# Seventeen more identity products on TensorE in the opening of a sorted-block attention kernel

## The chip, the cores and the metric

The kernel runs on one core of one Trainium2 chip. The metric is the device time of one execution in microseconds (us), as the median of several runs. A profile is one further execution, taken with its trace; times within it count from the first instruction.

## The reference, cut to what matters

Block-sorted attention, followed by a two-layer feed-forward part. The sorting matrix comes out of five rounds of row and column normalisation of `sort_net`; keys and values are mixed block by block with it; then each query block attends to its own sorted block.

```python
B, H, S, D = q.shape                       # 4, 8, 768, 64; 8 blocks of 96 rows
for _ in range(5):                         # P = sort_net, (4, 8, 8, 8)
    P = np.exp(P - np.max(P, axis=-1, keepdims=True))
    P = P / (np.sum(P, axis=-1, keepdims=True) + 1e-09)
    P = P / (np.sum(P, axis=-2, keepdims=True) + 1e-09)
k_sorted = np.einsum('bhij,bhjcd->bhicd', P, k_b)
v_sorted = np.einsum('bhij,bhjcd->bhicd', P, v_b)
scores = scale * np.matmul(q_b, k_sb.transpose(0, 1, 2, 4, 3))
attn = softmax(scores)                     # over the 96 keys of the block
x = np.matmul(attn, v_sb)                  # then (B*S, 512)
h = x @ w_in                               # 512 -> 2048
g = np.maximum(h, 0.0) + alpha * np.minimum(h, 0.0)
out = g @ w_out                            # 2048 -> 512
```

## The kernel before, in words

The work is cut into 32 pieces, g = 0 to 31: eight blocks in each of four batches. A piece is one block of 96 rows for all eight heads. Everything that the engines do is first recorded as operations in a graph (`G.add`), each with its engine, what it reads and what it writes. The order in which the engines take them is written out by hand: the table `SEQ` lists the numbers of all operations, and each engine runs its own in that order. `emit` then sets semaphore waits from the recorded reads and writes.

The opening of the program works on batch 0 (g = 0 to 7):

- `burst` (L888): 110 tiny products on zeros.
- `prep_q` (L600 on `hT`, which holds the loaded q of batch 0): six turnings of q into columns, evicted by ScalarE (ACT, L372) to `QTz`. The first is operation 89.
- `sinkhorn` on VectorE (DVE) and ACT gives the sorting matrix `Pb`; `spread0` (operation 79, L539) spreads it over the partitions, and L543 masks it to the block-diagonal `BDK`.
- `prep_k` (L600 on `KS`): six sorting products of k, evicted to `KT`; POOL pads `KT` (L642).
- `conv_v` (L653): copies on POOL and DVE that bring the loaded v into place in `hT`; `prep_v` (L674): eight sorting products of v, evicted to `VS`. The first is operation 114, the last operation 128.
- `attention(g)`: L715 (`s1`) makes scores, L721 takes their negated maxima `nm` on DVE; L736 and L727 (`s2`) make the turned scores and add `nm`; L759 exponentiates to `ET` on ACT; L768 (`o`) multiplies with `VS`; L776 and L779 divide on DVE to `xq`; L794 turns `xq`, and L372 evicts it to `xT`. Operation 158 is `s1` of g = 1; 162 is `o` of g = 1 (into `psYP`), 153 is `o` of g = 0 (into `psO`).

From then on the feed-forward part is woven in: `ffn1` (L823, `xT` times `w_in`, evicted by L833 and L836 to `hT`) and `ffn2` (L862, `hT` times `w_out`).

Beside this, the kernel has products whose result nobody reads: the identity matrix `identb` times itself repeated four times, 128 x 128 by 128 x 512, in bfloat16 (L808). The table `WARM` lists them: `89:10:y` puts ten ahead of operation 89 into the PSUM bank that the letter names (`y`: `psYP` at 0, `h`: `psH` at 0). `G.warm` inserts them into TensorE's order and has them wait for the identity, and for readers of the bank where there are any. Then comes the next entry of TensorE's order. All loads are issued by POOL; the queues of the other engines are not touched by `WARM`.

Of the kernel before, what the change touches and what calls it, by code (L numbers as in the profile page):

```python
# [29 lines left out]


WARM = """
89:10:y 79:7:y 93:2:y 104:2:y 114:7:y 158:2:y 153:2:h 205:1:y 207:1:y
"""

SEQ = """
# [993 lines left out]
```

## Time and profile before

| | |
|---|---|
| time, median of 3 runs | 239.45 us (238.71, 239.45, 241.29) |
| profiled execution, its own time | 238.55 us |
| its span, first to last instruction | 236.8 us |
| TensorE (PE) busy | 226.7 us, 96% of the span |
| DVE, ACT, POOL busy | 169.4, 151.7, 73.3 us |
| mean granted clock of PE | 0.992 |
| identity products (L808) | 38 |

The page gives busy time by engine, the span in forty slices, the chain that ended last, and groups of instructions by line. PE is the TensorE's products, PEld its weight loads. A row of the timeline has start, length, engine, line, operation, what is written and read, shapes and count; a bracket holds the idle time ahead of it and what ended it. The ends of products are modelled and include a tail, so that the next product may start ahead of a shown end.

### The profile page before, as it was taken

The page shows a single profiled execution, that of the slowest core. Times are in us where ns is not written, and L with a number is a line of the kernel's source. Part 1 is how long each engine was busy: PE and PEld are TensorE (multiplying, and loading weights), DVE is VectorE, ACT ScalarE, POOL GpSimd, SP SyncE. Part 2 cuts the span into 40 slices and gives each one's busy share as a digit, 9 for nine tenths or more (in the row PEclk, how much of TensorE's full clock was granted, in tenths as well). Part 3 has the DMA queues.
Part 4 walks back from the last instruction along what each step waited for, and adds up shares of the span by engine and source line. Part 5 has one row for each costly group of instructions (what it writes and reads, how often), then busy time and mean ns, then how long its engine had stood idle before and what let it go on. Part 6 is the DMA issues. An engine that isn't in the chain of part 4 may idle for free.

```text
span 236.8 us, 6180 instructions
## 1 busy us (share of the span) xinstructions
PE 226.7 (96%) x2474; PEld 142.7 (60%) x2503; DVE 169.4 (72%) x353; ACT 151.7 (64%) x423; POOL 73.3 (31%) x140
## 2 busy tenths in 40 slices
PE   7798899999999999999999999999999999999995
PEld 3346688687666666566655665655555555555544
DVE  4737688989899997869897667676766577644240
ACT  4465257587887988886768786756863646353232
POOL 7939824805879221148390020000000000000000
PEclk9999799999999999999999999999999999999999
DMA  5999999999999998999999797652442323400033
GB/s 95 214 214 212 205 219 195 173 212 162 181 92 145 141 168 125 154 182 194 130 100 92 210 157 157 98 95 42 125 106 69 97 50 84 132 3 0 1 136 133
DMA packets 70941, 31.36 MB, mean 132 GB/s; under 512 B 64504, under 2 KB 65280, under 8 KB 70912
## 3 DMA queue, kind: packets, MB, share of 16 engines
q0 software_dynamic: 22384, 13.63, 42.0%
q1 hardware_dynamic: 48528, 17.33, 36.9%
q8 instruction: 20, 0.33, 0.6%
q14 instruction: 9, 0.07, 0.1%
HBM read 27.28 MB, written 6.29 MB: 142 GB/s over the span
## 4 chain that ended last, share of the span: by engine, by line
PE 88%; DMA 5%; POOL 3%; DVE 2%; issue 1%; ACT 1%; POOLq 0%
PE psH L823 34%; PE psYP L862 30%; DMA VST<-in_v_dram 5%; PE psS L862 4%; PE psS L712 4%; PE psO L768 3%; PE psYP L669 2%; PE psYP L629 2%; PE psS L727 2%; PE psO L794 1%; PE psS L736 1%; PE psS L715 1%; POOL VDz L456 1%; POOL hT L653 1%; PE psH L808 1%
## 5 line engine op out<-in xcount | busy, mean ns | idle before, releaser
L836 DVE SCALAR_TENSOR_TENSOR hT<-t,omaT,psH 128x384 bf16<-128x384 f32 (+1 forms) x139 | 77.2, 571 | 36.3 <-ACT t L833 35.5
L823 PE MATMUL psH<-xT,w_in_bf 128*128 128x384 bf16 (+1 forms) x556 | 97.1, 311 | 0.0
L833 ACT ACTIVATE t<-psH 128x384 f32<-128x384 f32 (+1 forms) x139 | 62.9, 460 | 50.0 <-PE psH L823 47.7
L862 PE MATMUL psYP<-w_out_bf,hT 128*128 128x512 bf16 x308 | 77.6, 379 | 1.5
L823 PEld LDWEIGHTS psH<-xT,w_in_bf 128*128 128x128 bf16 x556 | 49.4, 98 | 29.4 <-DVE hT L836 2.1
L862 PEld LDWEIGHTS psYP<-w_out_bf,hT 128*128 128x128 bf16 x336 | 30.9, 98 | 28.2
L748 ACT ACTIVATE Esb<-psS,nf 96x96 bf16<-96x96 f32 x192 | 46.1, 345 | 2.0 <-DVE nf L721 2.0
L721 DVE TENSOR_REDUCE nf<-psS 96x8 f32<-96x768 f32 x24 | 22.8, 950 | 6.4 <-PE psS L712 6.0
L658 POOL COPY VDz<-VST 64x192 f32<-64x192 f32 x39 | 20.4, 523 | 19.2 <-DMA VST<-in_v_dram 13.5
L616 POOL COPY KSz<-KS 64x256 f32<-64x256 f32 x28 | 11.3, 404 | 33.6 <-PE psYP L629 21.2
L779 DVE TENSOR_TENSOR xq<-psO,rec 96x512 bf16<-96x512 f32 x31 | 21.2, 683 | 0.5
L401 POOL DMA_DIRECT2D QN<-in_q_dram x24 | 20.0, 838 | 2.3 <-DMA QTz<-QN 1.5
L712 PEld LDWEIGHTS psS<-KT,QTz 128*96 128x96 bf16 x192 | 12.1, 125 | 3.3
L768 PEld LDWEIGHTS psO<-VS,ET 112*128 112x128 bf16 x248 | 11.3, 99 | 3.9 <-ACT ET L759 0.5
L372 ACT ACTIVATE VS<-psYP 112x512 bf16<-112x512 f32 x15 | 10.3, 685 | 4.7 <-PE psYP L674 2.4
L768 PE MATMUL psO<-VS,ET 112*128 112x65 bf16 x248 | 13.0, 196 | 0.0
L712 PE MATMUL psS<-KT,QTz 128*96 128x96 bf16 x192 | 12.6, 208 | 0.0
L808 PE MATMUL psYP<-identb 128*128 128x512 bf16 x32 | 10.4, 460 | 0.5 <-ACT identb L372 0.5
L372 ACT ACTIVATE KT<-psYP 128x512 bf16<-128x512 f32 x15 | 8.9, 596 | 2.6 <-PE psYP L629 1.6
L372 ACT ACTIVATE outstg<-psYP 128x512 f32<-128x512 f32 x13 | 7.7, 604 | 3.2 <-PE psYP L862 3.2
L669 PEld LDWEIGHTS psYP<-BDV,VDz 128*128 128x128 bf16 x192 | 8.2, 98 | 2.4 <-ACT VS L372 0.2
L669 PE MATMUL psYP<-BDV,VDz 128*128 128x64 bf16 x192 | 9.5, 193 | 0.0
(137 smaller groups left out, 199.5 us busy)
## 6 DMA issues: line engine op xcount, KB each, us to landing
out_dram<-outstg SPq DMA_DIRECT2D x23, 256.0 KB, 2.4
KS<-in_k_dram POOLq DMA_DIRECT2D x3, 768.0 KB, 13.2
QN<-in_q_dram POOLq DMA_DIRECT2D x24, 96.0 KB, 4.7
w_in_bf<-in_moe_w_in_dram POOLq DMA_DIRECT2D x4, 512.0 KB, 16.0
w_out_bf<-in_moe_w_out_dram POOLq DMA_DIRECT2D x2, 1024.0 KB, 22.5
VST<-in_v_dram POOLq DMA_DIRECT2D x4, 384.0 KB, 17.2
hT<-in_q_dram POOLq DMA_DIRECT2D x1, 768.0 KB, 7.6
VST<-in_v_dram POOLq DMA_DIRECT2D x1, 768.0 KB, 11.5
```

The costliest lines, as they stand in the source:

```text
L372: return e.activation(o, i, ACTF.Copy) if e is nc.scalar else e.tensor_copy(o, i)
L658: G.add(SHIFT, lambda e, o2=o2, i2=i2: e.tensor_copy(o2, i2), {"dve": 424, "pool": 525}, r=vst, w=[("VDz", u % VSL, th)], prio=prio)
L669: inst = e.matmul(AP(t, off + dd * 64, [[row, 128], [1, 64]]), AP(VDz, (u % VSL * 4 + dd // 2) * 256 + dd % 2, [[VSL * 1024, 128], [2, 128]]),
L712: inst = e.matmul(o, AP(QTz[n], hp * 3072 + h4 * 768 + i * 96, [[6144, 128], [1, 96]]), AP(KT[n], (h4 * 8 + i) * bk, [[ld, 128], [64, 2], ...
L721: G.add(DVE, lambda e: e.tensor_reduce(AP(nx, 0, [[8, 96], [4, 2], [1, 4]]), AP(psX, 0, [[1024, 96], [512, 2], [96, 4], [1, 96]]), AxisLis ...
L748: inst = e.activation(AP(Esb[me], p * 128, [[1024, 96], [64, 2], [1, 48]]), AP(psX, (p // 4) * 512 + (p % 4) * 96, [[1024, 96], [48, 2], [ ...
L768: inst = e.matmul(AP(psZ, hp * 512 + h4 * 68, [[1024, 128], [1, 65]]), AP(ET[me] if far else ET[m], pos(h4, hp) * 96, [[800, nk], [1, 128] ...
L779: G.add(DVE, lambda e: e.tensor_tensor(out=AP(xq[me], 0, [[512, 96], [256, 2], [64, 4], [1, 64]]), in0=AP(psZ, 0, [[1024, 96], [512, 2], [ ...
L823: inst = e.matmul(AP(pt, poff, [[1024, 128], [1, n]]), AP(w_in_bf, kt * DFF + ft // 2 * 256 + ft % 2, [[KT_TILES * DFF, 128], [2, 128]]), ...
L833: G.add(ACT, lambda e: e.activation(AP(t1[tb], 0, [[384, 128], [1, n]]), AP(pt, poff, [[1024, 128], [1, n]]), ACTF.Relu, scale=-1.0), t_ac ...
L836: G.add(DVE, lambda e: e.scalar_tensor_tensor(out=AP(hT, ft * RING + tok % RING, [[FT_TILES * RING, 128], [1, n]]), in0=AP(t1[tb], 0, [[38 ...
L862: inst = e.matmul(AP(bank[0], bank[1], [[1024, 128], [1, n]]), AP(hT, ft * RING + tok % RING, [[FT_TILES * RING, 128], [1, 128]]), AP(w_ou ...
```

## The change

The counts of six places in `WARM` are raised, and two places are new. The operations, their data and the order of all others stay.

```diff
 WARM = """
-89:10:y 79:7:y 93:2:y 104:2:y 114:7:y 158:2:y 153:2:h 205:1:y 207:1:y
+89:14:y 79:8:y 93:2:y 104:2:y 114:9:y 158:6:y 153:3:h 205:1:y 207:1:y 128:4:y 162:1:y
 """
```

Four more stand ahead of operation 89, one more ahead of 79, two ahead of 114, four ahead of 158, one ahead of 153; new are four ahead of 128 and one ahead of 162: seventeen.

TensorE's order (the only one that differs), where v's first sorting product (L674) follows k's last (L600) and the first scores of g = 1 (L715) come; the names behind the operation are the tile written and the tiles read:

```order
 L600 MATMUL psH<-BDK,KS 64x64 x32
 L600 MATMUL psO<-BDK,KS 64x64 x32
-L808 MATMUL psYP<-identb 128x512 x7
+L808 MATMUL psYP<-identb 128x512 x9
 L674 MATMUL psO<-BDK,hT 64x64 x16
-L808 MATMUL psYP<-identb 128x512 x2
+L808 MATMUL psYP<-identb 128x512 x6
 L715 MATMUL psH<-KT,QTz 96x96 x8
 L674 MATMUL psYP<-BDK,hT 64x64 x16
```

Two more products stand ahead of L674 and four more ahead of L715. Further on, TensorE from v's last sorting products to the two output products (L768), before the change:

```order
L674 MATMUL psO<-BDK,hT 64x64 x48
L736 MATMUL psS<-QTz,KT 112x96 x8
L727 MATMUL psS<-identb,nm 112x96 x8
L768 MATMUL psYP<-VS,ET 128x65 x8
L808 MATMUL psH<-identb 128x512 x2
L768 MATMUL psO<-VS,ET 128x65 x8
L808 MATMUL psH<-identb 128x512 x4
```

and with it:

```order
L674 MATMUL psO<-BDK,hT 64x64 x32
L808 MATMUL psYP<-identb 128x512 x4
L674 MATMUL psO<-BDK,hT 64x64 x16
L736 MATMUL psS<-QTz,KT 112x96 x8
L727 MATMUL psS<-identb,nm 112x96 x8
L808 MATMUL psYP<-identb 128x512
L768 MATMUL psYP<-VS,ET 128x65 x8
L808 MATMUL psH<-identb 128x512 x3
L768 MATMUL psO<-VS,ET 128x65 x8
L808 MATMUL psH<-identb 128x512 x4
```

The last of v's three sorting products in this place now comes behind four identity products, the output product of g = 1 behind one, and that of g = 0 behind three instead of two.

## The prediction

> **What bounds the kernel now.** I read the page first: the shares of the engines, the clock that TensorE (PE) was granted in each fortieth of the span, and the shares of the chain that ended last.
>
> ```profile
> PE 226.7 (96%) x2474; PEld 142.7 (60%) x2503; DVE 169.4 (72%) x353; ACT 151.7 (64%) x423; POOL 73.3 (31%) x140
> PEclk9999799999999999999999999999999999999999
> PE 88%; DMA 5%; POOL 3%; DVE 2%; issue 1%; ACT 1%; POOLq 0%
> ```
>
> PE is the bound, and one slice out of forty, the fifth (23.7 to 29.6 us), has less than a full clock. The rest of the chain lies mostly in the opening. The chain in order of time, over the opening, shows what sets the pace there:
>
> ```profile
> 5.45 11.47 DMA VST<-in_v_dram
> ...
> 19.68 0.38 PE psH L715 x8
> ...
> 27.00 0.85 PE psH L808 x2
> ```
>
> Until 19.6 us the load of v and POOL's copies set the end; PE only fills waits. From 24.60 on the chain stays on PE, identity products (L808) among it. Busy time by stage, in stretches cut at the places where the clock changes, and at last the long rest:
>
> ```profile
> 18.00:21.41 3.41, 2.43 (x88) 1.74 (x83) 2.37 (x6) 1.31 (x3) 3.09 (x6) 1.00 1.04 211
> 21.41:24.82 3.41, 2.50 (x79) 2.14 (x75) 2.51 (x5) 2.18 (x3) 2.95 (x8) 1.00 1.05 210
> 24.80:24.85 0.05, 0.05 (x14) 0.05 (x10) 0.00 (x0) 0.00 (x0) 0.00 (x0) 0.75 0.81 164
> 28.20:28.25 0.05, 0.05 (x3) 0.04 (x1) 0.00 (x0) 0.00 (x0) 0.02 (x1) 0.62 1.89 369
> 32.00:232.00 200.00, 198.42 (x1868) 124.21 (x1895) 149.31 (x284) 136.56 (x391) 48.60 (x90) 1.00 0.78 123
> ```
>
> After the length of a row come PE, PEld, DVE, ACT and POOL; the third number from the end is the clock. A slice at 0.75 is half full and half at 0.50, so the clock falls to half at 24.825; by the 0.62 it is back at 28.24. That is 3.41 us at half speed, worth at most 1.71 us. From 32 to 232 us PE is busy 99% at full clock: nothing there swallows a shift, so what PE gains or loses by 32 us reaches the end one to one.
>
> **Fifteen of the seventeen products: do they fit in waits?** PE's timeline, with the wait ahead of a row in brackets:
>
> ```profile
> 2.80 4.45 PE L808 MATMUL psYP<-identb 128*128 128x512 bf16 x10 [0.53 <-ACT identb L372]
> 8.92 0.44 PE L600 MATMUL psS<-identb,hT 64*64 64x64 bf16 x16 [1.68 <-DMA hT<-in_q_dram]
> ...
> 10.55 1.69 PE L808 MATMUL psYP<-identb 128*128 128x512 bf16 x7
> 12.42 0.37 PE L539 MATMUL psYP<-Pb,sel 32*128 32x8 bf16 x8 [0.18 <-DVE Pb L532]
> ...
> 15.62 1.68 PE L808 MATMUL psYP<-identb 128*128 128x512 bf16 x7
> 16.95 0.34 DVE L653 COPY hT<-VST 128x192 f32<-128x192 f32 x1 [2.52 <-DMA VST<-in_v_dram]
> 17.70 0.45 PE L674 MATMUL psO<-BDK,hT 128*64 128x64 bf16 x16 [0.41 <-POOL hT L653]
> 18.09 0.60 PE L808 MATMUL psYP<-identb 128*128 128x512 bf16 x2
> 19.68 0.38 PE L715 MATMUL psH<-KT,QTz 64*96 64x96 bf16 x8 [0.98 <-POOL KT L642]
> ...
> 24.60 0.52 PE L674 MATMUL psO<-BDK,hT 128*64 128x64 bf16 x16 [0.88 <-DVE VS L372]
> ```
>
> Two products last 0.60 and seven 1.69, so one more costs (1.69 - 0.60)/5 = 0.218 us; of a run's shown time 0.16 is the tail of the last, which the next product does not wait for. The first ten (4.45) step by 0.425: the array runs at half speed there too, although the page shows 9 (its clock record has not begun). Place by place, with the tail added to the wait shown:
>
> - ahead of the first turning: 4 x 0.425 = 1.70, wait 1.68 plus tail, so 14 products from 2.80 leave the array at 8.75, q comes at 8.92.
> - ahead of L539: 0.22 against 0.18 + 0.16.
> - ahead of the first L674: 0.44 against 0.41 + 0.16.
> - ahead of L715: 4 x 0.218 = 0.87 against 0.98 + 0.16.
> - ahead of the last L674: 0.87 against 0.88 plus a tail.
>
> So all fifteen cost nothing at full clock, with 0.1 to 0.3 us left at each place; what hides them are DMAs, POOL copies and evictions, which don't depend on them. Were the cover gone at one place, it would cost 0.2 to 0.9. Only PE's order changes; no other queue is moved past anything.
>
> **What they do to the clock.** The trace has no record of what decides it, so I bound it. The stretch that ended in the fall holds as much busy PE time (2.50) as the one before it, which kept full clock (2.43); but the same stretches, with the identity products alone, read
>
> ```profile
> 18.00:21.41 3.41, 0.60 (x2) 0.11 (x2) 1.00 1.04 211
> 21.41:24.82 3.41, 0.00 (x0) 0.00 (x0) 1.00 1.05 210
> ```
>
> The one that kept its clock has two of them, of 512 columns each; the one that fell has only products of 8 to 96 columns, whose shown time is mostly tail. With four identity products ahead of the last L674 the weak stretch gets 0.87 us of solid streaming, twice what was enough in the one before. I take it that the fall at 24.825 goes. Bounds: it stays (gain 0, and the products below are paid at half speed), or all of the 1.71 comes back.
>
> The Trainium skill, "TensorE: Matmul & The Clock Gate", section "Why this matters for your kernels", asks only for no PE-idle gaps over some 3 us; the trace disagrees, since the longest wait in the stretch before the fall is 0.88 us. By that rule idle time did not cause the fall, the four products would not remove it, and the sum would be that of the second rival below.
>
> **The stretch at full clock.** Rows at half speed, and the same kinds of work at full speed later:
>
> ```profile
> 25.05 0.61 PE L736 MATMUL psS<-QTz,KT 64*112 64x96 bf16 x8
> 25.16 0.70 DVE L372 CAST VS<-psO 112x512 bf16<-112x512 f32 x1 [0.61 <-PE psO L674]
> 25.58 0.98 PE L727 MATMUL psS<-identb,nm 96*112 96x96 bf16 x8
> 26.36 0.64 PE L768 MATMUL psYP<-VS,ET 112*128 112x65 bf16 x8
> 26.60 0.81 ACT L759 ACTIVATE ET<-psS 112x768 bf16<-112x768 f32 x1 [2.15 <-PE psS L727]
> 26.81 1.04 PE L808 MATMUL psH<-identb 128*128 128x512 bf16 x2
> 27.65 0.65 PE L768 MATMUL psO<-VS,ET 112*128 112x65 bf16 x8
> 28.11 1.09 PE L808 MATMUL psH<-identb 128*128 128x512 bf16 x4
> 29.31 0.35 PE L794 MATMUL psO<-identb,xq 96*128 96x96 bf16 x4
> 30.30 0.83 PE L823 MATMUL psH<-xT,w_in_bf 128*128 128x192 bf16 x8
> 31.06 0.41 PE L736 MATMUL psS<-QTz,KT 64*112 64x96 bf16 x8
> 31.40 0.61 PE L727 MATMUL psS<-identb,nm 96*112 96x96 bf16 x8
> 31.84 0.49 PE L823 MATMUL psYP<-xT,w_in_bf 128*128 128x192 bf16 x4
> 32.04 0.81 ACT L759 ACTIVATE ET<-psS 112x768 bf16<-112x768 f32 x1 [0.32 <-PE psS L727]
> ```
>
> L736 and L727 together take 1.31 at half speed (25.05 to 26.36) and 0.78 at full (31.06 to 31.84). With L674 at 24.60 and its sixteen done in 0.28 (an estimate, from 0.39 at 17.70 less the time to start): L736 at 24.88, L727 at 25.22, the added product at 25.66, over at 25.88. L768 on psYP also needs the VS eviction, which ends at 25.86 today and about 25.80 then: the added product costs 0.02. Eight L768 take 0.45 at half, 0.23 at full: 26.11. Three products: 26.77. L768 on psO needs ET, which starts 0.64 after L727 at full clock (31.40 to 32.04), so runs 25.86 to 26.67: the third product costs 0.10. L768 on psO at 26.77 instead of 27.65, 0.88 earlier. The division into xq and L794 follow it by 1.66 today (27.65 to 29.31), about 0.1 less at full clock: 28.33. L823, the first product of the feed-forward part, comes 0.99 after that: 29.32 instead of 30.30, **0.98 earlier**.
>
> **What is late next.** L823 also waits for w_in. Its four loads, by tile:
>
> ```profile
> L907 POOL DMA_DIRECT2D w_in_bf<-in_moe_w_in_dram x4: 528/536/548, 7.5 to 10.9; - x4
> DMA to landing us min/median/max: 15.0/16.0/18.9
> ```
>
> The last is issued at 10.9, and if it is the one that takes 18.9, it lands at 29.8; the DMA share is 1.04 and 1.05 in the stretches above, so a faster PE brings it no sooner. L823 starts then at about 29.86 (DVE's copy above began at 16.95, 0.03 after v had landed by the chain, 5.45 + 11.47): 0.44 of the 0.98 is left, the rest turns into a wait for w_in. Sum: 238.55 - 0.44 = **238.1 us** for the profiled execution (span 236.8, and 1.75 around it).
>
> The three timed runs lie 0.16, 0.90 and 2.74 above that execution. Something varies by more than the whole term here. I take the smallest of the three on top, 238.1 + 0.16 = **238.3**, since a fall of the clock that comes at another place in another run is what the added products would also take out; with the median's 0.90 it would be 239.0. In the Trainium skill, same page, section "What's actually happening", the window of 3413 ns that sets the clock runs free of the kernel's start; 3.41 us at half speed agrees, that it moves between runs no run here shows. By it, the time would be 238.3 rather than 239.0.
>
> **Rivals.**
> - *Full carry.* w_in lands earlier than I read (the 18.9 belongs to an earlier issue: then 26.4 to 28.8). All 0.98 arrives: 237.6, or 237.7 with the 0.16. Against it: four loads in one queue tend to land in order. Chance 0.12.
> - *The clock falls all the same* (slower). The decision looks at something the four products don't feed, and the stretch from 24.8 stays at half. Then the fall costs what it does now, and two products are new on the path at 0.425 each: today L768 on psO starts at 27.65 though its ET was done at 27.41, so both are paid: 238.55 + 0.85 = 239.4, up to 240.3 with the median's 0.90. It decides if the clock is still 0.50 after 24.8. If half speed also covers 17 to 24 us, four products ahead of L715 last 1.70 against 1.14 of room, and four ahead of the last L674 1.70 against 1.04: another 1.2, 240.6, and 241.5 with the 0.90. Chance 0.20, of which 0.07 over 1% slower.
> - *No effect on the end.* PE's gain is swallowed by w_in altogether (landing at 30.2) or by DVE, whose reductions (L721) pace the two blocks after 30 us: 238.5 to 239.4. Chance 0.18.
>
> **How the numbers follow.** My forecast, 238.3, has 0.50, and by itself 237.9 to 239.0. Both ends move into the other cases: low 237.5 (full carry), high 240.0 (clock falls all the same, less its worst half); outside is about 0.15. One per cent, 2.4 us, is about what a measurement of this kernel can tell from no change. Faster by that needs under 237.1: full carry and a low run together, 0.10. Slower needs over 241.8, the second rival at its worst in a run like the slowest of the three: 0.07. Within: 0.83.
>
> **What would show it.** Right: 1.00 in the clock from 7.8 us to past 30, the fifth slice a 9; L715 still at 19.7, L674 still at 24.6; L768 on psO near 26.8; PE idle by about 0.5 us ahead of the first L823, released by the DMA of w_in, at 29.9. Wrong: a stretch at 0.50 that is still there or has moved; L715 or the last L674 later than now, with no wait left ahead of it; L823 at 29.3 with no wait.

## The result, and the profile after

| | before | after |
|---|---|---|
| median, 22 executions of each | 239.92 us (238.36 to 242.46) | 238.28 us (237.78 to 244.75) |
| profiled execution, its own time | 238.55 us | 238.30 us |
| its span | 236.8 us | 236.6 us |
| mean granted clock of TensorE (PE) in it | 0.992 | 1.000 |

The ratio is 0.9944, with a 95% interval of 0.992 to 0.9969: faster by half a per cent. The ratios here are formed without executions far above their kernel's fastest; medians and counts include them.

The page of after, its busy time of PE and the chain's shares, and the core's clock:

```profile
PE 228.6 (97%) x2491; PEld 143.4 (61%) x2520; DVE 169.5 (72%) x353; ACT 151.8 (64%) x423; POOL 73.4 (31%) x140
PE 91%; DMA 3%; DVE 2%; issue 1%; ACT 1%; POOLq 0%
```

```profile
core 0: 236.6 us, clock 1.000
```

Seventeen products (2474 to 2491) added 1.9 us of busy PE, and the span fell by 0.2. The opening, in the prediction's stretches (PE, PEld, DVE, ACT, POOL, clock, DMA share, GB/s):

```profile
18.00:21.41 3.41, 3.41 (x93) 2.31 (x92) 2.32 (x4) 0.70 (x2) 3.03 (x7) 1.00 1.05 214
21.41:24.82 3.41, 3.38 (x74) 2.39 (x74) 2.22 (x5) 2.17 (x3) 2.93 (x7) 1.00 1.08 215
24.82:28.24 3.42, 3.42 (x48) 2.27 (x47) 3.22 (x8) 0.81 (x1) 2.96 (x7) 1.00 1.04 210
32.00:232.00 200.00, 198.25 (x1868) 124.31 (x1895) 148.73 (x284) 136.56 (x391) 48.64 (x90) 1.00 0.78 123
```

and the identity products alone in the two that stand ahead of the old fall:

```profile
18.00:21.41 3.41, 1.44 (x6) 0.47 (x6) 1.00 1.05 214
21.41:24.82 3.41, 1.04 (x4) 0.31 (x4) 1.00 1.08 215
```

Where the clock was 0.50 from 24.8 to 28.2 us it is now 1.00. PE's timeline through the places that the prediction went over:

```profile
8.85 0.44 PE L600 MATMUL psS<-identb,hT 64*64 64x64 bf16 x16 [0.75 <-DMA hT<-in_q_dram]
...
17.59 0.45 PE L674 MATMUL psO<-BDK,hT 128*64 128x64 bf16 x16
17.97 1.47 PE L808 MATMUL psYP<-identb 128*128 128x512 bf16 x6
19.37 0.38 PE L715 MATMUL psH<-KT,QTz 64*96 64x96 bf16 x8
...
23.35 1.04 PE L808 MATMUL psYP<-identb 128*128 128x512 bf16 x4
24.32 0.45 PE L674 MATMUL psO<-BDK,hT 128*64 128x64 bf16 x16
24.70 0.41 PE L736 MATMUL psS<-QTz,KT 64*112 64x96 bf16 x8
25.03 0.61 PE L727 MATMUL psS<-identb,nm 96*112 96x96 bf16 x8
25.48 0.38 PE L808 MATMUL psYP<-identb 128*128 128x512 bf16 x1
...
26.60 0.41 PE L768 MATMUL psO<-VS,ET 112*128 112x65 bf16 x8
...
28.03 0.34 PE L794 MATMUL psO<-identb,xq 96*128 96x96 bf16 x4
...
28.80 0.28 PE L560 MATMUL psYP<-Pb,selk 32*64 32x64 bf16 x6
30.09 0.82 PE L823 MATMUL psH<-xT,w_in_bf 128*128 128x192 bf16 x8 [1.01 <-issue]
```

The trace of after records no change of the clock at all, so the products have to bear out the 1.00: L736 and L727 together take 0.78 us (24.70 to 25.48), where they took 1.31 before. The waits of 0.41, 0.98 and 0.88 us ahead of L674, L715 and the last L674 are gone; L768 on psO starts 1.05 us earlier (27.65 to 26.60), L794 1.28 earlier (29.31 to 28.03). Then PE stands idle for 1.01 us ahead of the first L823. The view says "issue", which means that it shows no releaser. The loads of w_in, by tile, tell what it was:

```profile
L907 POOL DMA_DIRECT2D w_in_bf<-in_moe_w_in_dram x4: 531/534/551, 7.5 to 10.9; - x4
DMA to landing us min/median/max: 15.1/16.1/19.0
```

Issued at 10.9 and landed 19.0 later is about 29.9 to 30.0; L823 starts right behind it, at 30.09, against 30.30 before. In all seven traces with w_in by rows in which L823 starts between 30.04 and 30.26, it does so 0.09 us behind w_in's last landing (29.95 to 30.17). Of more than a microsecond only 0.21 us is left there, 0.2 in the span, 0.25 in the execution's time. The chain of after, around the identity products and at this wait:

```profile
15.61 2.05 PE psYP L808 x9
...
18.04 1.40 PE psYP L808 x6
...
29.08 1.01 issue
30.09 0.82 PE psH L823 x8
```

The identity products now lie on the chain themselves, ahead of L674 and of L715. v landed earlier in this execution (below), so that PE, not v, came last at both places. It costs nothing at the end, since the chain then waits for w_in.

The profiled executions differ by 0.25 us, the medians by 1.64. So the time is not told by the one fall of the clock that the prediction worked on.

### The profile page after: what moved, and what is told of

Read it like the earlier page. It is cut to its first block, busy times and chain, and to the rows that moved or that the text cites. A ratio compares the mean times of both kernels' runs of the same rounds, so it can differ in the third digit from the quotient of the medians.

```text
span 236.6 us, 6214 instructions
## 1 busy us (share of the span) xinstructions
PE 228.6 (97%) x2491; PEld 143.4 (61%) x2520; DVE 169.5 (72%) x353; ACT 151.8 (64%) x423; POOL 73.4 (31%) x140
## 4 chain that ended last, share of the span: by engine, by line
PE 91%; DMA 3%; DVE 2%; issue 1%; ACT 1%; POOLq 0%
PE psH L823 34%; PE psYP L862 29%; PE psS L862 4%; PE psS L712 4%; PE psYP L808 3%; PE psO L768 3%; DMA hT<-in_q_dram 3%; PE psYP L669 2%; PE psYP L629 2%; PE psS L727 2%; PE psO L794 1%; PE psS L736 1%; PE psS L715 1%; PE psO L674 1%; PE psO L862 1%
## 5 line engine op out<-in xcount | busy, mean ns | idle before, releaser
L823 PE MATMUL psH<-xT,w_in_bf 128*128 128x384 bf16 (+1 forms) x556 | 96.9, 311 | 1.2 <-issue 1.0
L862 PE MATMUL psYP<-w_out_bf,hT 128*128 128x512 bf16 x308 | 77.6, 379 | 1.5
L823 PEld LDWEIGHTS psH<-xT,w_in_bf 128*128 128x128 bf16 x556 | 49.5, 98 | 30.4 <-DVE hT L836 1.9
L862 PEld LDWEIGHTS psYP<-w_out_bf,hT 128*128 128x128 bf16 x336 | 30.9, 98 | 28.2
L808 PE MATMUL psYP<-identb 128*128 128x512 bf16 x48 | 14.2, 433 | 0.5 <-ACT identb L372 0.5
L768 PEld LDWEIGHTS psO<-VS,ET 112*128 112x128 bf16 x248 | 11.1, 98 | 3.6 <-ACT ET L759 0.3
L768 PE MATMUL psO<-VS,ET 112*128 112x65 bf16 x248 | 12.7, 194 | 0.0
```

The source lines that it names most:

```text
L768: inst = e.matmul(AP(psZ, hp * 512 + h4 * 68, [[1024, 128], [1, 65]]), AP(ET[me] if far else ET[m], pos(h4, hp) * 96, [[800, nk], [1, 128] ...
L808: inst = e.matmul(AP(bank[0], bank[1], [[1024, 128], [1, 512]]), identb[:, :], AP(identb, 0, [[128, 128], [0, 4], [1, 128]]))
L823: inst = e.matmul(AP(pt, poff, [[1024, 128], [1, n]]), AP(w_in_bf, kt * DFF + ft // 2 * 256 + ft % 2, [[KT_TILES * DFF, 128], [2, 128]]), ...
L862: inst = e.matmul(AP(bank[0], bank[1], [[1024, 128], [1, n]]), AP(hT, ft * RING + tok % RING, [[FT_TILES * RING, 128], [1, 128]]), AP(w_ou ...
```

## The experiments

A mean granted clock of 0.993 is one stretch of 3.41 us at half speed (half of 3.41 in a span of 236.8 is 0.007), 0.986 is two, 1.000 is none. Such a stretch is called a window below, and executions are counted by their mean clock. It counts falls alone: time ahead of the first recorded change passes as full speed, though the first products run at half speed (steps of 0.427 us). So a late first rise of the clock does not show in it. Kernels of one group ran on one chip beside executions of before, 32, 29 and 35 of them, with medians of 240.1, 240.09 and 240.26 us. Of these 96, 2 had no stretch at half, 11 had one, 77 two, and 6 more than two. Of the 22 of after, 15 had none (237.78 to 238.56 us), 4 one (239.82 to 244.18), 3 two (241.83 to 244.75).

The theory to be tested was that of the prediction: the four products ahead of operation 128 keep the clock, and w_in's last landing then sets when the feed-forward part starts. Its rivals: other places, or all seventeen, keep the clock; something else than w_in swallows the gain; the gate, which grants the clock, looks at streaming time and not at how much of the array works.

**The four alone.** Before, with one new place:

```diff
-... 158:2:y 153:2:h 205:1:y 207:1:y
+... 158:2:y 153:2:h 205:1:y 207:1:y 128:4:y
```

> The kernel before with only the four products ahead of v's last sorting product added (4 of the 17). Theory A (these four fill the weak stretch that made the clock fall): where the run is timed like the profiled one, the clock stays full, L823 starts at w_in's landing near 30.0 and the time is 238.3, the same as with all seventeen. Rival B (the clock goes by the whole opening, all seventeen are needed): the clock still falls in most runs, mean granted clock 0.993 or 0.986, the time 239.4 to 239.9 like before. Between them: the four mend one place, and in runs where the clock's stretches are cut elsewhere the fall comes further ahead, from 17 us on; then the times split into 238.3 and 239.5 to 241.

Measured: 240.96 us (12 executions, 238.44 to 242.28), ratio 1.003 (0.9997 to 1.0062). Eleven of the twelve had two stretches at half (0.984 to 0.986). The four products by themselves do not keep the clock in the usual execution; where its two stretches lay no trace shows. In the profiled one, which had none (238.44), the timeline shows something else, a stop of PE in the middle of v's sorting products:

```profile
23.95 0.36 PE L674 MATMUL psO<-BDK,hT 128*64 128x64 bf16 x10 [0.56 <-issue]
...
30.26 0.82 PE L823 MATMUL psH<-xT,w_in_bf 128*128 128x192 bf16 x8 [0.33 <-issue]
```

**All but the four.** After, without `128:4:y`:

```diff
-... 205:1:y 207:1:y 128:4:y 162:1:y
+... 205:1:y 207:1:y 162:1:y
```

> The changed kernel without the four products ahead of v's last sorting product (thirteen stay). Theory A: the stretch from 21.4 to 24.8 us has no identity product again, the clock falls behind it in most runs, and the two products added in the stretch behind are paid at half speed: 239.4 to 240.3. Rival B (the other thirteen keep the clock up): clock 1.00, 238.3.

Measured: 239.4 us (12; 238.0 to 241.76), ratio 0.9964 (0.9936 to 0.9992): four with no stretch at half (238.0 to 238.86), five with one (239.09 to 239.70), three with two (240.29 to 241.76). The thirteen others take out about one stretch of the two; with the four added, both are gone more often (15 of after's 22). So neither part alone does what both do; the single places were not tried. Each stretch at half goes with about 1 us here.

**w_in by columns.** w_in's four loads brought 128 of its rows each, so the first L823 needed all four. Cut by columns, it needs only the first. On after:

```diff
-            AP(w_in_bf, p * DFF, [[KT_TILES * DFF, 128], [1, DFF]]),
-            AP(moe_w_in.tensor, p * 128 * DFF, [[DFF, 128], [1, DFF]])),
+            AP(w_in_bf, p * 512, [[KT_TILES * DFF, 128], [DFF, KT_TILES], [1, 512]]),
+            AP(moe_w_in.tensor, p * 512, [[DFF, 128], [128 * DFF, KT_TILES], [1, 512]])),
...
-  [("w_in", kt) for kt in range(KT_TILES)]
+  [("w_in", ft // 4)]
```

> The changed kernel with the four loads of w_in cut by columns instead of rows, so that the first feed-forward products need the first load only (landed near 22.6 us), the same bytes in the same place of the queue. Theory A (the first L823 is held by w_in's last landing, 1.0 us of idle PE in the profile after): L823 starts near 29.1 instead of 30.1, and 0.8 to 1.0 us arrive at the end: 237.3 to 237.5. Rival C (DVE or a later transfer swallows it: the wait only moves to the next block): 238.3, with the wait ahead of L736 or L823 on psYP near 31 us.

Measured: 237.78 us (10; 237.57 to 241.91), ratio 0.9903 (0.9872 to 0.9935). Eight had no stretch at half, seven of them between 237.57 and 237.85. Against the 238.1 that is usual for after at full clock, the wait for w_in was worth 0.4 to 0.5 us of the 1.0 shown. The profiled execution is one of the other two, and shows what happened in it:

```profile
22.29 0.38 PE L674 MATMUL psO<-BDK,hT 128*64 128x64 bf16 x11
25.34 0.75 PE L674 MATMUL psO<-BDK,hT 128*64 128x64 bf16 x21 [2.67 <-issue]
```

```profile
24.30:31.00 6.70, 5.66 (x67) 3.51 (x67) 1.90 (x5) 1.49 (x2) 5.50 (x9) 0.50 1.21 209
```

PE stops for 2.67 us inside a run of 32 like products, and the clock is at half for two windows (24.2 to 31.1 us), from within the stop on.

**The same on before.** The same two edits, on the kernel before:

> The kernel before with the loads of w_in cut by columns. Theory A: PE came to L823 at 30.3 there, after w_in had landed at 29.8, so w_in held nothing: unchanged, 239.9, and up to 0.5 less in runs whose clock falls elsewhere. Rival C: unchanged as well. A gain of 1 us here would say that cutting the loads helps by itself (a quicker transfer) and that the run before it says nothing of w_in.

Measured: 239.98 us (12; 238.89 to 240.6), ratio 0.9979 (0.9953 to 1.0005), all twelve with two stretches at half. Where the clock falls, PE comes to L823 no earlier than w_in (31.16 us in the profiled execution), and there is little to win. Its windows show two falls, as many as the mean clock counts in a usual execution of before, of which there is no trace:

```profile
6.50:9.90 3.40, 1.30 (x52) 0.81 (x52) 2.45 (x14) 0.69 (x4) 3.23 (x7) 1.00 1.02 208
10.10:13.30 3.20, 3.20 (x50) 1.76 (x47) 1.79 (x9) 3.16 (x8) 3.20 (x7) 0.50 1.05 213
23.60:27.00 3.40, 1.83 (x51) 1.62 (x51) 2.03 (x5) 0.99 (x2) 3.00 (x6) 1.00 1.24 205
27.10:30.40 3.30, 3.30 (x22) 1.66 (x20) 1.89 (x5) 0.40 (x1) 2.89 (x6) 0.50 1.20 212
```

Behind the idle wait for q (1.30 us busy of 3.40) the clock is at half from about 10 us; behind v's sorting products (1.83 of 3.40, with a stop in it) from about 27. The four products that the change puts ahead of the first turning stand in the wait of the first, the four ahead of the last L674 in that of the second. Which place takes out which fall was not tried one by one; with the four ahead of the last L674 alone, eleven of twelve executions still count two falls. In every trace with recorded changes, these lie a whole number of windows apart, while the first lies anywhere: at 6.59 us here, 7.76 in the profile of before, and from 4.79 to 7.55 in the others with whole identity products in the opening. So the cut of the windows, which the prediction could not see move, differs from execution to execution; that it decides which of them lose the clock is likely, and not shown.

**Few cells.** Does the gate look at the time that PE streams, or at how much of the array works? After, with every identity product on a 32 x 32 corner, the columns unchanged:

```diff
-            inst = e.matmul(AP(bank[0], bank[1], [[1024, 128], [1, 512]]), identb[:, :], AP(identb, 0, [[128, 128], [0, 4], [1, 128]]))
+            inst = e.matmul(AP(bank[0], bank[1], [[1024, 32], [1, 512]]), identb[0:32, 0:32], AP(identb, 0, [[128, 32], [0, 4], [1, 128]]))
```

> The changed kernel with every identity product of that helper cut to a 32 x 32 corner of the array: same count, same places, same 512 columns and so the same time on TensorE, a sixteenth of the cells at work. Theory A (the clock goes by how long products stream): clock 1.00 in most runs and 238.1 to 238.3, as with whole products. Rival D (it goes by the share of the array at work): the weak stretches are weak again, the clock falls once or twice or comes up late, 0.993 to 0.97, and 240 to 243.

Measured: 253.45 us (6; 247.49 to 254.87), 13.4 above before beside it; no interval was formed. In its timeline,

```profile
2.81 6.15 PE L808 MATMUL psYP<-identb 32*32 32x512 bf16 x14 [0.54 <-ACT identb L372]
...
12.03 3.59 PE L808 MATMUL psYP<-identb 32*32 32x512 bf16 x8
...
47.34 0.69 PE L823 MATMUL psH<-xT,w_in_bf 128*128 128x192 bf16 x4
47.96 0.38 PE L808 MATMUL psYP<-identb 32*32 32x512 bf16 x1
```

the fourteen stream without a gap for 6.15 us, and eight still take 3.59 where after's eight, on the whole array, take 1.90. Half speed lasts until about 47.7 us, although PE is busy for 44.5 of the 44.9 us ahead of it; from 47.96 one product takes 0.38, the full-speed time. The record of the clock starts only there, so the page shows full speed throughout, and three of the six executions have a mean of 1.000 at 253 to 254 us. Rival D has the direction right, and its 240 to 243 was far too low. So streaming time alone does not bring the clock; the share of the array at work counts. No run shows how much of it is enough. The Trainium skill, "TensorE: Matmul & The Clock Gate", section "What's actually happening", says that the gate follows how busy PE has been; that agrees with this run only if a product on one sixteenth of the cells counts as hardly busy.

**Where the stops belong.** The stops in the profiles of the four alone, of all but the four (0.45 us) and of both kernels with w_in by columns lie at one place in the program: behind instruction 960 of those that the trace records on TensorE, counted from 0, with products, weight loads and the records of semaphores and drains together. (Products and weight loads alone give 953 here, and 955 in the next run.) In the kernels before and after, the products on both sides of the same number start 0.22 and 0.23 us apart. The transfers of instructions, sixteen KB each, are a queue of their own on the page (20 of them, 0.33 MB), and PE resumes about 1.4 to 1.5 us after the end of one: in the four alone one ends at 22.43 and PE resumes at 23.95, with w_in by columns 23.75 and 25.17 on before, 23.89 and 25.34 on after. If the stop is at a number and not at some work, 32 more tiny products ahead of everything move it to other work. After, with

```diff
-BURST = 110
+BURST = 142
```

> The changed kernel with 142 instead of 110 of the tiny products at the very start, which end before the identity is ready and cost no time, but move every later instruction of TensorE by 64 places. In all profiles so far TensorE stops for 0.2 to 2.9 us at its 960th recorded instruction, in the middle of v's sorting products, some 1.45 us behind a 16 KB transfer of the instruction queue. Theory E (it waits there for its next 256 instructions): the stop moves to the same instruction number, 64 instructions earlier in the work, where the transfer has had 6 us instead of 4.5, and is gone; fewer runs whose clock falls; 237.9 to 238.2 with hardly a run over 239.5 (seven of 22 were, with the change alone). Rival F (the stop belongs to the work at that place, a wait on a buffer): it stays at the same product, and the times spread as before.

Measured: 239.94 us (12; 238.86 to 243.3), ratio 0.9992 (0.9966 to 1.0019); seven had full clock, at 238.86 to 240.07, some 1 to 1.5 us above the 15 of after. In its timeline the stop has moved ahead in the work by 64 records (32 products and their weight loads), into the products on psYP:

```profile
20.89 0.42 PE L674 MATMUL psYP<-BDK,hT 128*64 128x64 bf16 x14
22.11 0.22 PE L674 MATMUL psYP<-BDK,hT 128*64 128x64 bf16 x2 [0.80 <-issue]
```

It is again behind instruction 960, and behind 704 two products start 0.30 us apart. The work around them is other work, so the number decides, against rival F; but theory E also expected the stop to go and the time to shorten, and neither happened. The extra microsecond is not the stops' in the profiled execution: L823 starts at 30.17, 0.08 later than in after, and the half microsecond in its span (237.1 against 236.6) comes far behind the opening:

```profile
206.59 1.46 PE L823 MATMUL psH<-xT,w_in_bf 128*128 128x384 bf16 x8 [0.44 <-DVE hT L836]
```

Why the others are longer stays open.

**The same on before.** `BURST = 142` on the kernel before:

> The kernel before with 142 tiny products at the start. Theory E: the stop in v's sorting products goes, about 0.2 to 1 us less; the weak stretches of the clock stay, so 0.986 in most runs and 239.3 to 239.8 instead of 240.1. If the stop alone made the clock fall: 1.00 and 238.3. Rival F: unchanged, 240.1.

Measured: 240.79 us (12; 237.95 to 243.25), ratio 0.9973 (0.9937 to 1.0009), above the 239.3 to 239.8 of theory E and not told apart from before, with clocks from 0.971 to 0.993. The profiled execution (237.98) had one stretch at half, the early one:

```profile
5.90:9.30 3.40, 1.04 (x22) 0.41 (x22) 2.45 (x13) 0.62 (x3) 3.23 (x9) 1.00 1.03 210
9.40:12.70 3.30, 3.30 (x87) 2.50 (x82) 2.24 (x11) 2.51 (x7) 3.30 (x7) 0.50 1.07 220
```

No stop stands in its timeline. L823 started at 30.04, after 0.77 us of idle time, as in after: in this execution the early fall was hidden by later loads, and cost nothing.

**Everything together.** After, with w_in by columns, `BURST = 142`, and the four products in two pairs:

```diff
-... 128:4:y 162:1:y
+... 126:2:y 128:2:y 162:1:y
```

> The changed kernel with w_in loaded by columns, 142 tiny products at the start, and two of the four products ahead of v's last sorting product moved ahead of the last but one. Theories A and E together: L823 no longer waits for w_in and the stop is gone, L823 near 29.0 and 237.2 to 237.5 in nearly all runs, clock 1.00. If only 0.4 of w_in's 1.0 us arrives, as the times of the run with w_in by columns suggest: 237.6 to 237.8, and the profile shows what takes its place between L560 and L736.

Measured: 239.96 us (12; 238.51 to 242.49), ratio 0.9991 (0.9958 to 1.0023): a miss, nothing gained. The stops came behind recorded instructions 704 and 960, 256 apart:

```profile
16.17 0.47 PE L600 MATMUL psO<-BDK,KS 64*64 64x64 bf16 x18 [0.47 <-issue]
...
23.17 0.22 PE L674 MATMUL psYP<-BDK,hT 128*64 128x64 bf16 x2 [0.81 <-issue]
```

With these 1.28 us of idle time ahead of it, L823 starts at 31.04, later than w_in needs: what the early w_in could bring is spent on the stops.

**Without the burst's change.** The same, with `BURST` at 110, beside the kernel after itself:

> The changed kernel with w_in loaded by columns, and two of the four products ahead of v's last sorting product moved ahead of the last but one; the start as it was (110 tiny products). Theory A: L823 starts as soon as TensorE comes to it, about 29.1 where the clock is full, 0.9 earlier than in the profile after, and what doesn't arrive at the end shows as a wait right behind. Times of full clock: 237.6 as with w_in by columns alone. Rival: the two products ahead of the last but one delay its eviction, L768 on psYP comes 0.2 to 0.4 later, and 238.0.

> The changed kernel once more, beside the others on one chip: 238.1 to 238.3 where the clock is full (two runs in three), 239.8 to 244 in the others.

Measured: 237.98 us (12; 237.32 to 244.03), ratio 0.9921 (0.988 to 0.9963), and 238.48 us for after (12; 237.82 to 242.04), ratio 0.9945 (0.991 to 0.9981). At full clock, seven executions lie between 237.32 and 238.13, and nine of after's between 237.82 and 239.61, with a tenth at 242.04. The timelines, first of this kernel, then of after beside it:

```profile
28.71 0.84 PE L823 MATMUL psH<-xT,w_in_bf 128*128 128x192 bf16 x8
...
35.67 0.81 PE L862 MATMUL psYP<-w_out_bf,hT 128*128 128x512 bf16 x3 [0.54 <-DMA w_out_bf<-in_moe_w_out_dram]
```

```profile
30.07 0.82 PE L823 MATMUL psH<-xT,w_in_bf 128*128 128x192 bf16 x8 [0.60 <-issue]
```

L823 starts 1.36 us earlier, with no wait, which shows that the "issue" of after was w_in. Then w_out is late, its first load landed at 35.4 (issued at 12.3, landed 23.1 later). The lead is 0.86 at the first L862, 0.65 at 43 us, and some 0.4 from 134 us to the end. The gain of 1.36 is taken in part by the next load and in part, I think, by pieces that VectorE paces; the latter was not tried. This and w_in by columns alone (237.78) are the best versions here; the runs don't tell the two apart, and the ratios' intervals overlap with that of after.

**A shorter burst.** After, with `BURST = 35`, which moves the stops the other way:

> The changed kernel with 35 instead of 110 tiny products at the start: 150 instructions fewer ahead of all the rest. Theory E (TensorE waits for its next 256 instructions at fixed instruction numbers): the stop that was at the 960th recorded instruction now falls at other work, some 150 instructions later, near 27 us, where products are longer and the transfer has had 6 us; stops then of 0 to 0.5, and more runs at full clock, 238.1. If the tiny products were what brings the clock up: it comes up a stretch later, past 10 us, and the time is up by 0.5 to 1.

Measured: 238.65 us (12; 238.21 to 239.91), ratio 0.9947 (0.9924 to 0.9971); ten had full clock, two had one stretch at half. Its stop:

```profile
20.41 0.24 PE L715 MATMUL psS<-KT,QTz 64*96 64x96 bf16 x1
21.08 0.34 PE L715 MATMUL psS<-KT,QTz 64*96 64x96 bf16 x7 [0.43 <-issue]
```

It is behind instruction 704; at 960, now among the identity products near 27 us, none shows. No execution was above 239.91, where after's went to 244.75. The median is as after's, and the scatter above is smaller; twelve executions don't prove that.

**No opening products at all.** After, with only the two late places left:

```diff
-89:14:y 79:8:y 93:2:y 104:2:y 114:9:y 158:6:y 153:3:h 205:1:y 207:1:y 128:4:y 162:1:y
+205:1:y 207:1:y
```

> The changed kernel without any of the table's identity products in the opening (49, of which 32 were there before; four others, ahead of the turning of xq, stay). Theory A: TensorE's work alone is too thin until 25 us, the clock comes up only there or later, every turning and sorting product is paid at half speed, L823 starts near 32 and the time is 241 to 243. If the clock came up on its own with the first turnings: 239.5 to 240.

Measured: 245.34 us (12; 241.38 to 249.08), ratio 1.0109 (1.0069 to 1.0149). Its windows:

```profile
16.10:22.80 6.70, 5.11 (x137) 4.50 (x130) 4.43 (x11) 3.59 (x8) 5.78 (x11) 0.50 1.05 214
26.30:36.50 10.20, 9.56 (x90) 7.32 (x90) 5.57 (x15) 2.66 (x5) 3.86 (x7) 0.50 1.10 213
```

In the second stretch PE is busy 9.56 of 10.20 us, and still at half speed: busy time alone does not bring the clock back. The median is above the 241 to 243 expected, and 6.9 us above after's beside it (238.48); by the ratios (1.0109 against 0.9945) the difference is 3.9 us. In the profiled execution (245.11) not all of it arises in the opening. L823 starts at 32.67, 2.58 later than in after; from 42 us PE is 4.3 behind, and the rest of 6.8 comes later, mostly in these waits:

```profile
110.57 0.41 PE L669 MATMUL psYP<-BDV,VDz 128*128 128x64 bf16 x8 [1.31 <-POOL VDz L658]
140.46 0.81 PE L823 MATMUL psH<-xT,w_in_bf 128*128 128x384 bf16 x4 [0.85 <-DVE nf L721]
```

In this execution, then, some 4 us are lost in the opening itself; whether the later waits follow from it no run shows.

## Why the prediction was right, and where it was not

The number was right: 238.3 forecast, 238.28 measured, and a gain of under 1%, as forecast. That it agrees to 0.02 us is luck: the sum gave 238.1 for the profiled execution, which took 238.30, and the 0.16 on top came from one of three timed runs. By its own steps:

- *Fifteen products fit in waits.* Right in effect. L715 began at 19.37, not later than 19.68, and the last L674 at 24.32. The room that was computed did not hold: v came earlier, as VectorE's copy shows (16.95 before),

```profile
16.32 0.34 DVE L653 COPY hT<-VST 128x192 f32<-128x192 f32 x1 [1.97 <-DMA VST<-in_v_dram]
```

  and the products themselves were last at two places. That w_in comes later hid this. The fourteen left PE earlier than the 8.75 forecast (0.75 us of wait is left ahead of 8.85), since the clock came up within them.
- *The fall at 24.825 goes.* It did in the profiled execution, and 25 of 34 of after's have full clock. **The reason was the step that failed.** The prediction put it down to the four products ahead of the last L674, 0.87 us of streaming, "twice what was enough"; with those alone, eleven of twelve executions kept two falls. A usual execution of before has two falls, near 10 and near 27 us in the one trace that shows two. The profiled execution on which the sum was made had only one, and was an exception. It takes the four and the thirteen together.
- *More streaming over the whole array, not busy time, keeps the clock.* Right in direction, and shown by the few cells: the same columns through a corner of the array left half speed until 47.7 us. What is enough it could not say, nor do the runs.
- *The stretch at full clock.* Right: 26.77, 28.33 and 29.32 were forecast for L768 on psO, L794 and L823; L768 and L794 came at 26.60 and 28.03, and PE was free for L823 at 29.08.
- *w_in is late next.* Right as a mechanism. The size was off: 0.44 us was to be left, 0.21 was. w_in's last load landed at about 30.0 instead of 29.8, and L823 followed at 30.09 instead of 29.86. In the profiles of the other kernels with w_in by rows and full clock ahead of it, L823 comes at 30.04 to 30.26, so the difference lies within the scatter of a load. Given an earlier w_in, L823 did come 1.36 us earlier.
- *After 32 us one to one.* Right for these 0.2 us: 0.21 at L823, 0.2 in the span. For the longer lead of 1.36 it is wrong, as w_out and later pieces took nearly 1.0 of it.
- *238.3 and not 239.0.* The assumption that falls at another place in another run would be taken out as well carried the number, and it was right: 15 of 22 executions of after, and 10 of the 12 later ones, have full clock; of before, 2 of 96. Most of the median's gain of 1.64 us should come from there, while the sum's own term was 0.44: beside the experiments, before has a median of 240.13 with two falls and 239.17 with one. Its two executions without a fall (238.82 and 239.63) are too few to say what is left.

Of the rivals, full carry did not happen. The clock that falls all the same happened in 7 of the 22, at 239.8 to 244.8 where 239.4 to 241.5 had been priced; the part above may be stops of PE, which the prediction knew nothing of: the one profile of such an execution, that of w_in by columns on after, has one of 2.67 us. A first rise of the clock that comes late would do it too, unseen by the mean clock: one of after's took 242.04 at 0.999. That w_in swallows all was nearly so in the profiled execution.

## What to carry to other kernels

Before a sum is made on a profile's single fall of the clock, look at the mean clocks of many executions: the profiled one may be an exception, and the median's gain lies in how often the clock falls. Check such a mean by the step of a known product, since it leaves out the time ahead of the first recorded change. Filler products on the whole array kept the clock here, and the same columns on a sixteenth of it did not; put as many as the waits take. Where PE is freed, look for the next load's landing, cut that load so that the first use needs only a part, and then look again.

## What the runs showed of the hardware that was not expected

- PE stops by itself at fixed numbers of its program: behind recorded instructions 704 and 960, 256 apart, for up to 2.67 us, 1.3 to 1.6 us behind the end of a transfer of instructions. Without the opening's products, too, a stop (0.44 us) stands behind 960, there in L736. The stop moved with the count of instructions and not with the work. The view calls it "issue", as it does the wait for w_in; a count of instructions and a tile's landing tell the two apart. The Trainium skill, "Runtime: NRT & Kernel Launch", section "Instruction fetch mechanics", has blocks of 16 KiB and 256 instructions, which agrees with the 256 here; that crossing them is mostly hidden does not, in an opening whose DMA share is above 1 (1.02 to 1.24 in the rows above). Why the stop is long in one execution and not in the other stays open.
- Behind the two long stops (1.89 and 2.67 us, both kernels with w_in by columns) the clock was at half for one window and for two; behind stops of up to 0.81 us it stayed full in the profiles of kernels with products in the opening.
- What makes the clock fall in the remaining quarter of after's executions stays open (no trace shows one; with w_in by columns one shows the stop of 2.67 us), as does how much of the array is enough.
